# The inputs of the attention loaded at the end of a period, and one pair's sums made a period later

## The chip, the core and the metric

The kernel runs on one core of a Trainium2 chip. The metric is device time in microseconds (us). Before the change the median of three runs is 1099.42 us (1099.28 to 1099.94). The execution that the profiler recorded, from which all rows below come, took 1100.56 us; its first to its last instruction span 1098.8 us of that.

## The reference

Retention attention with 4 batches, 8 heads, 768 positions and a head size of 64, and two feed-forward layers over its 3072 tokens (model size 512, hidden size 2048), all in fp32:

```python
for t in range(S):
    state = gamma * state + einsum('bhd,bhe->bhde', k[:, :, t], v[:, :, t])
    y[:, :, t] = scale * einsum('bhd,bhde->bhe', q[:, :, t], state)
x = y.transpose(0, 2, 1, 3).reshape(B * S, H * D)
h = x @ w_in;  g = maximum(0.01 * h, h);  x = g @ w_out
h = maximum(x @ w_in2, 0);                out = (h * h) @ w_out2
```

## The kernel before

TensorE multiplies numbers split into a high and a low part, so that a product takes three matmuls (high by high, low by high, high by low). From the second block of tokens on, the products of a layer are done with seven products of half-size quarters instead of eight; the sums and differences of quarters of a weight that this takes are called its units. They are made once on VectorE (DVE) and ScalarE (ACT), written to DRAM and read back by the blocks that use them.

The tokens go in three blocks of 1024 (b = 0, 1, 2). A layer's 2048 hidden columns go in eight **periods** (q = 0 to 7) of two tiles of 128. Layer 0 of blocks 0 and 1 is interleaved with the attention of the positions that the later blocks need. One call of attend() in a period scores one pair of heads of a batch, finishes the values of the pair before it, prepares the next one and has the one after that loaded. Names in the rows:

- r: the loaded q, k and v of a pair (load_pair, two DMAs out of the input named first, three buffers each); vs and qs are its scaled parts (L193 on ACT, L183 on DVE), sc its scores, y its values, xs the values turned into the input of the layer.
- sg and st: raw weights in 64-bit words; L402, L403 on ACT and L404, L405, L408 on DVE turn them into fp32. In block 0 a period takes two sg tiles.
- wraw, wflt: fp32 weights kept in DRAM by block 0. In block 1 load_in(q + 2) loads wf from wraw (one buffer), and L506 on ACT and L507 on DVE split it and its sums (L520 to L523) into wa and wb. wid holds the units stored for later blocks; read_out(q + 1) loads wo, the units of the second product's weights, from wou.
- pa, pb, pd, acc: PSUM tiles. L716 copies the products of the first matrix, L742 to L756 add and activate them, and gh, gl (L797, L798) are the activated values that the second product (acc) takes.
- of: units of layer 1's second weights. make_units (L619) reads a pair of hidden tiles from wflt, all_units writes four plain quarters (L596 on ACT, L597 on DVE, wou on the GpSimd queue) and sum_units the four sums (L606 to L609, then L596 and L597 again). both_block (L958) steps these generators between the products of layer 1.

TensorE's instructions, every load (SyncE's queue, SP) and every store (GpSimd's queue, POOL) are pinned in the order in which the program is written: mm, load and store (L130 to L137) each wait for the one before on their queue. An issue whose buffer isn't free holds all that stand behind it on its queue. What ACT and DVE do is put in order by a scheduler that works on a model of the time, so a changed load can also change their order; on the chip both engines then take it in that order.

In block 0 the period ends with load_w (one or two sg); in block 1 with load_in and read_out. The loads of a pair's r are issued inside attend, ahead of those.

Of the kernel before, what the change touches and what calls it, by code (L numbers as in the profile page):

```python
# [30 lines left out]
NQ = NJ // 2  # L31
# [31 lines left out]
def retention_then_two_mlps(  # L63
# [66 lines left out]
    def mm(**kw):  # L130
        pin(nc.tensor.matmul(**kw))  # L131

    def load(**io):
        pin(nc.sync.dma_start(**io))
# [165 lines left out]
    n_load, n_prep, n_score, n_done = [0], [0], [0], [0]  # L300

    def loads_to(n):
        while n_load[0] < min(n, len(ups)):
            load_pair(ups[n_load[0]])
            n_load[0] += 1
# [19 lines left out]
        if last:  # L325
            prep_to(n_score[0] + 1)

    def attend(last):

        n, prev = n_score[0], ups[n_done[0]]  # L330
        if n < last:
            prep_to(n + 1)
            scores(ups[n], False, prev if n_done[0] < n and prev[0] < (NC - 1) * B else None)
            n_score[0] += 1
        if n_done[0] < n:
            values(prev)
            n_done[0] += 1
        prep_to(min(n_score[0] + 1, last))
        loads_to(min(n_done[0] + 3, n_score[0] + 2))

# [15 lines left out]
    def load_w(q, half):  # L358
        if q == NQ:
            return  # L360
        t = stage[q, half] = w_p.tile([P, 1024], U64, tag="sg", name="sg", bufs=2)
        load(out=t, in_=w1[q, half])
# [589 lines left out]
    def both_block(lay, b, here):  # L952

        nl, nb = (lay, b + 1) if b + 1 < NB else (1, 0) if not lay else (None, None)
        pa = None
        for n in range(NQ + 1):
            f = first_half(lay, b, n) if n < NQ else iter(())
            r = second_half(lay, b, n - 1, pa) if n else iter(())  # L958
            if (lay, b) == (1, 0) and 3 <= n <= 6:
                with aside():  # L960
                    next(here[n // 5], None)
            if (lay, b) == (1, 0) and n == NQ - 1:
                with aside():
                    next(made, None)
            for k in range(4):
                pa = next(f, None)
                if n == NQ - 1 and k < 2:
                    read_stage(lay, 0, (2 * k, 2 * k + 1))
                if lay == 0 and n and (k == 1 or k == 3 and n in (1, 2, 4, 5)):
                    with aside():  # L970
                        next(here, None)
                if k < 3:
                    next(r, None)
            if n == NQ - 1:
                read_stage(lay, 1, range(4))
            for q, k in UNITS[0 if not lay else 1 if b else 2].get(n, ()):
                read_units(lay, q, k)
            if (lay, b) == (1, 0) and n < NQ - 1 and n != 5:
                if n == 0:
                    v = quarters() + scratch("ss", "ss", "wb", "wf")  # L980
                else:
                    with aside():
                        next(made, None)
                if n in (0, 2, 4):
                    made = make_units(5 + n // 2, *v[:5])
                    next(made)
                    if n == 0:
                        here = [units_here(4, v[5], v[7]), units_here(6, v[6], v[5])]
                        for m in here:
                            next(m)  # L990
        A = [ps["acc"].tile([P, T], F32, tag=f"acc{m}", name="acc") for m in range(2)]
        s = {}
        steps = None if nl is None else operands(nl, nb)
        at = {4: (7, 13), 5: (5, 11), 6: (1, 5, 9)} if lay else {4: (13,), 5: (5, 11), 6: (1, 4, 8, 12)}
        for n, i in enumerate(STAGES):
            if i in (5, 2):
                Dd = [ps["acc"].tile([P, T], F32, tag=f"acc{2 + m}", name="acc") for m in range(2)]
            bank = Dd if i in (5, 3, 2) else A
            if i == 4:
                order = [(q, m) for m in range(2) for q in range(NQ)]  # L1000
            else:
                order = [(q, m) for q in range(NQ) for m in range(2)]
            for e, (q, m) in enumerate(order):
                r = rot[i, q]
                for k, (l, h) in enumerate(((0, 0), (1, 0), (0, 1))):
                    mm(
                        out=bank[m], lhsT=units[i, q // 2][:, q % 2, l, m * P:(m + 1) * P], rhs=r[:, h],
                        start=i in (1, 5, 2) and q == 0 and k == 0, stop=q == NQ - 1 and k == 2, skip_group_check=True,
                    )
                if e % 2 and n + 1 < len(STAGES):  # L1010
                    prepare(STAGES[n + 1], q)
                if e == 1:
                    if 1 <= n <= 5:
                        read_stage(lay, n + 1, range(4))
                    if n == (1 if lay else 3) and nl is not None:
                        read_x(nb)
                    if n in (3, 5) and lay and nl is not None:
                        read_units(1, (n - 3) // 2)
                    if n == 6 and nl is not None:
                        read_units(1, 2, 0, True)  # L1020
                if lay == 0:
                    if (n, e) in ((0, 1), (0, 9), (0, 15)):
                        with aside():
                            next(here, None)
                    if (n, e) in ((1, 1), (2, 13)):
                        made = units_here(n - 1, x_p.tile([P, 1024], F32, tag="xh4", name="of"))
                        next(made)
                    if n in (2, 4) and e in (3, 9):
                        with aside():
                            next(made, None)  # L1030
                if steps and e in at.get(n, ()):
                    with aside():
                        next(steps, None)
            if i in (1, 5):
                s[i] = late["r"].tile([P, 2, T], F32, tag="ss", name="ss", bufs=2)
            elif i == 6:
                s[i] = x_p.tile([P, 2, T], F32, tag="xl4", name="ss")
            elif i == 4:
                s[i] = w_p.tile([P, 2, T], F32, tag="wb", name="ss")
            for m in range(2):  # L1040
                if i in (1, 5, 6) or (i == 4 and m == 0):
                    nc.scalar.copy(s[i][:, m], bank[m])
                elif i == 4:
                    nc.vector.tensor_copy(s[i][:, m], bank[m])
                else:
                    y = s[{3: 6, 7: 5, 2: 1}[i]][:, m]
                    nc.vector.tensor_tensor(out=y, in0=y, in1=bank[m], op=ALU.add)
            if i in (3, 7, 2, 4):
                y, mh, t = {3: (s.get(6), 0, 1), 7: (s.get(5), 1, 1), 2: (s.get(1), 0, 0), 4: (s.get(4), 1, 0)}[i]
                for m in range(2):  # L1050
                    put = load if not lay or nl is None and i == 4 else store
                    put(out=(out if lay else ydr)[b][:, 2 * mh + m, t * T:(t + 1) * T], in_=y[:, m])
# [115 lines left out]
    for b in range(NB - 1):  # L1168
        rest = (b + 2) * B * NP
        for q in range(NQ):  # L1170
            more = 0 < q < NQ - 1
            if b == 0:
# [13 lines left out]
                emit_plain(q, 1, 1)  # L1186
                if more:
                    put_out(b, 2 * q - 1)
                attend(rest)
            else:  # L1190
                part = emit_in(0, b, q)
                next(part)
# [5 lines left out]
                    next(new, None)  # L1198
                if more:
                    put_out(b, 2 * q - 1, (0, 6))  # L1200
                attend(rest)
                next(part)
                with aside() if q and q > 6 else ExitStack():
                    next(new, None)
# [4 lines left out]
                    pass  # L1209
            if q + 1 < NQ:  # L1210
                if b == 0:
                    loads_to(n_done[0] + 3)
                    if q:
                        plain_in(q + 1)
                        if q + 2 < NQ:
                            load_w(q + 2, 0)
                        for n in (q - 1,) if q < 5 else (4, 5) if q == 5 else (6,):
                            out_sums(n)
                    with aside(), tc.issue_after(paired[q]):
                        make_out(q + 1)  # L1220
                    if q + 2 < NQ:
                        if q == 0:
                            load_w(q + 2, 0)
                        load_w(q + 2, 1)
                else:
                    if q + 2 < NQ:
                        load_in(q + 2)
                    read_out(q + 1)
            elif b == 0:
                out_sums(NQ - 1)  # L1230
            if b == 0 and q > 1:
# [117 lines left out]
```

## Time and profile before

| | |
|---|---|
| median of three runs | 1099.42 us |
| profiled execution | 1100.56 us, span 1098.8 us, mean granted TensorE clock 0.997 |
| TensorE busy | 1082.4 us, 99% of the span |
| VectorE busy | 763.4 us, 69% |
| ScalarE busy | 611.6 us, 56% |
| moved by DMA | 293.31 MB, 267 GB/s over the span |

Busy time of TensorE is as long as its matmuls at the clock that was granted, so a matmul at half the clock counts as busy for longer. Of ACT and DVE a third to a half is idle; that they are idle in the mean does not say that they are in time at a given place.

### The profile page before, as it was taken

Reading aid. Unit: us, or ns where it says so; the run is one execution under the profiler, and the core shown is the slowest. Engines: PE = TensorE matmul, PEld = TensorE weight load, DVE = VectorE, ACT = ScalarE, POOL = GpSimd, SP = SyncE. Lnnn points to the kernel's source line nnn. Section 1 sums busy time; section 2 is a strip of 40 time slices with the busy share of each in tenths; the row PEclk is TensorE's granted clock in tenths of the full one; section 3 lists DMA queues with packets and bytes.
Section 4 is the critical chain, followed back from the end, with each engine's and each line's share of the span. In section 5 each row is a group of like instructions: output and inputs, shape, how many; then the busy total and the mean of one; then the engine's idle time right before and its main releaser. Section 6 shows DMA issues by size and latency. Waiting matters only on the chain.

```text
span 1098.8 us, 15540 instructions
## 1 busy us (share of the span) xinstructions
PE 1082.4 (99%) x5599; PEld 862.5 (78%) x5599; DVE 763.4 (69%) x1333; ACT 611.6 (56%) x1111; POOL 87.2 (8%) x146
## 2 busy tenths in 40 slices
PE   9999999999989999999999999999999999999998
PEld 6787787777767777787788887888888888888886
DVE  5888997676755656658797968877555868456853
ACT  5757775554545554357665567655455555455542
POOL 0011111101000000012101012100000001000000
PEclk9999999999989999999999999999999999999999
DMA  9689998878797957679978778978335876447571
GB/s 373 211 332 331 355 337 311 290 267 298 249 341 247 344 202 248 231 289 377 375 265 290 287 264 278 399 261 344 116 135 198 318 255 230 155 148 260 167 241 58
DMA packets 81660, 293.31 MB, mean 267 GB/s; under 512 B 8368, under 2 KB 10928, under 8 KB 74032
## 3 DMA queue, kind: packets, MB, share of 16 engines
q1 hardware_dynamic: 62400, 214.00, 54.9%
q0 software_dynamic: 19040, 78.13, 18.3%
q8 instruction: 44, 0.72, 0.3%
q14 instruction: 32, 0.26, 0.1%
q10 hardware_dynamic: 144, 0.20, 0.1%
HBM read 206.31 MB, written 85.98 MB: 266 GB/s over the span
## 4 chain that ended last, share of the span: by engine, by line
PE 83%; DMA 6%; DVE 5%; issue 3%; ACT 2%; POOL 1%; SPq 0%; POOLq 0%; DVEq 0%; ACTq 0%
PE acc L131 40%; PE pa L131 23%; PE pd L131 7%; PE y L131 5%; PE pb L131 4%; PE sc L131 4%; DMA of<-wflt 2%; DMA wb<-wid 1%; DMA wf<-wraw 1%; DMA wid<-wa 1%; DMA wflt<-sf 1%; DVE rot L877 1%; PE idle L131 1%; DVE wa L507 0%; DVE xl L673 0%
## 5 line engine op out<-in xcount | busy, mean ns | idle before, releaser
L131 PE MATMUL acc<-rot,wu 128*128 128x512 f32 x1344 | 314.3, 395 | 0.0
L131 PEld LDWEIGHTS acc<-rot,wu 128*128 128x128 f32 x1344 | 252.3, 188 | 61.3
L131 PE MATMUL pa<-xh,wa 128*128 128x512 f32 x464 | 143.7, 391 | 0.0
L876 ACT CAST rot<-gu 128x512 fp32r<-128x512 f32 x160 | 99.0, 620 | 77.1 <-PE acc L131 67.8
L877 DVE TENSOR_TENSOR rot<-gu,rot 128x512 fp32r<-128x512 f32 x160 | 109.1, 688 | 46.7 <-ACT rot L876 46.1
L131 PE MATMUL pa<-xh,wb 128*128 128x512 f32 x432 | 135.9, 395 | 4.3 <-DVE wb L432 2.3
L131 PE MATMUL acc<-gh,wo 128*128 128x512 f32 x400 | 107.4, 401 | 3.8 <-ACT gh L797 3.8
L131 PEld LDWEIGHTS pa<-xh,wa 128*128 128x128 f32 x464 | 87.1, 188 | 19.5 <-DMA wa<-wid 0.4
L131 PE MATMUL pd<-xh,wa 128*128 128x512 f32 x320 | 99.0, 390 | 1.8 <-DVE wa L507 1.5
L131 PEld LDWEIGHTS pa<-xh,wb 128*128 128x128 f32 x432 | 79.7, 188 | 24.7 <-DVE wb L432 2.6
L131 PEld LDWEIGHTS acc<-gh,wo 128*128 128x128 f32 x400 | 75.1, 190 | 22.9 <-ACT gh L797 4.6
L131 PE MATMUL pa<-xl,wa 128*128 128x512 f32 x232 | 90.5, 390 | 0.0
L131 PE MATMUL pa<-xl,wb 128*128 128x512 f32 x216 | 84.2, 390 | 0.0
L131 PEld LDWEIGHTS pd<-xh,wa 128*128 128x128 f32 x320 | 60.0, 188 | 15.2 <-DVE wa L507 1.9
L877 DVE TENSOR_TENSOR rot<-gt,rot 128x512 fp32r<-128x512 f32 x64 | 44.2, 691 | 30.7 <-ACT rot L876 30.3
L131 PE MATMUL pd<-xl,wa 128*128 128x512 f32 x160 | 62.3, 389 | 0.0
L876 ACT CAST rot<-gt 128x512 fp32r<-128x512 f32 x64 | 39.6, 621 | 39.0 <-PE acc L131 36.2
L131 PE MATMUL acc<-gl,wo 128*128 128x512 f32 x200 | 57.7, 396 | 0.0
L723 ACT ACTIVATE gt<-gt 128x512 f32<-128x512 f32 x48 | 30.4, 633 | 47.7 <-DVE gt L904 33.1
L798 DVE TENSOR_TENSOR gl<-g,gh 128x512 fp32r<-128x512 f32 x50 | 34.1, 688 | 30.5 <-ACT gh L797 14.7
L916 DVE TENSOR_TENSOR gu<-gu,pb 128x512 f32<-128x512 f32 x32 | 22.0, 687 | 44.1 <-PE pb L131 44.0
L131 PEld LDWEIGHTS pa<-xl,wa 128*128 128x128 f32 x232 | 43.5, 188 | 9.2
(152 smaller groups left out, 1715.4 us busy)
## 6 DMA issues: line engine op xcount, KB each, us to landing
wu<-wou SPq DMA_DIRECT2D x112, 512.0 KB, 6.1
wa<-wid SPq DMA_DIRECT2D x28, 1024.0 KB, 6.0
wou<-of POOLq DMA_DIRECT2D x48, 512.0 KB, 6.5
wb<-wid SPq DMA_DIRECT2D x28, 768.0 KB, 6.5
wo<-wou SPq DMA_DIRECT2D x20, 1024.0 KB, 6.5
sg<-w SPq DMA_DIRECT2D x16, 1024.0 KB, 7.3
r<-first SPq DMA_DIRECT2D x50, 256.0 KB, 5.7
st<-w SPq DMA_DIRECT2D x24, 512.0 KB, 7.6
```

The source lines that it names most:

```text
L131: pin(nc.tensor.matmul(**kw))
L723: nc.scalar.activation(out=g, in_=g, func=AF.Relu)
L798: mark[1] = seq(nc.vector.tensor_tensor(out=gl, in0=g, in1=gh.bitcast(F32), op=ALU.subtract)).ins
L876: mark[0] = nc.scalar.copy(r[:, 0], s).ins
L877: mark[1] = nc.vector.tensor_tensor(out=r[:, 1], in0=s, in1=r[:, 0].bitcast(F32), op=ALU.subtract).ins
L916: nc.vector.tensor_tensor(out=u[:, 0], in0=u[:, 0], in1=pb, op=ALU.add)
```

## The change

Two edits. First, attend takes the number of pairs to load ahead as an argument; in the periods of blocks 0 and 1 it is 2 and not 3, so that attend there issues no load, and the loads of the next pair come at the end of the period: behind load_w in block 0, behind load_in and read_out in block 1 (not in the last period of a block). Second, in layer 1 of block 0 the step of make_units is left out in n = 4 and not in n = 5, and the generator for pair 7 starts in n = 5 and not 4, so that the last sums of pair 6 are made one period later.

```diff
-    def attend(last):
+    def attend(last, more=3):
...
-        loads_to(min(n_done[0] + 3, n_score[0] + 2))
+        loads_to(min(n_done[0] + more, n_score[0] + 2))
...
-            if (lay, b) == (1, 0) and n < NQ - 1 and n != 5:
+            if (lay, b) == (1, 0) and n < NQ - 1 and n != 4:
...
-                if n in (0, 2, 4):
+                if n in (0, 2, 5):
                     made = make_units(5 + n // 2, *v[:5])
...
-                attend(rest)
+                attend(rest, 2)
             else:
...
-                attend(rest)
+                attend(rest, 2)
...
                 if b == 0:
-                    loads_to(n_done[0] + 3)
                     if q:
                         plain_in(q + 1)
...
                         load_w(q + 2, 1)
+                    loads_to(n_done[0] + 3)
                 else:
                     if q + 2 < NQ:
                         load_in(q + 2)
                     read_out(q + 1)
+                    loads_to(n_done[0] + 3)
```

No matmul, cast or byte is added or taken away, and TensorE's order is the same. On SP the loads stand in another order. In block 0 the two r of a period go behind its two sg:

```order
-L134 DMA r<-first 128x512 x2
-L134 DMA sg<-w 128x1024 x2
-L134 DMA st<-w 128x512
-L134 DMA r<-first 128x512 x2
-L134 DMA sg<-w 128x1024 x2
+L134 DMA sg<-w 128x1024 x2
+L134 DMA r<-first 128x512 x2
+L134 DMA st<-w 128x512
+L134 DMA sg<-w 128x1024 x2
+L134 DMA r<-first 128x512 x2
```

The sg loads of a period are now issued ahead of its r. In block 1, from the first period on (wraw_105 and the wo behind it), the two r go behind wf and wo:

```order
-L134 DMA r<-first 128x512
-L134 DMA r<-first 128x384
 L134 DMA wflt_0_112<-sf 128x512
 L134 DMA wf<-wraw_105 128x1024
 L134 DMA wo<-wou_123 128x4x512
+L134 DMA r<-first 128x512
+L134 DMA r<-first 128x384
 L134 DMA wflt_0_118<-sf 128x512
 L134 DMA st<-w 128x512
 L134 DMA wf<-wflt_0_106 128x512
-L134 DMA r<-first 128x512
-L134 DMA r<-first 128x384
```

So the r of a period is three issues later on the queue, and the next wf and wo are no longer behind it. On ACT the order in the first period of block 1 is the one of before, but for the r that vs names (r_2801 before, r_2851 now); this is the order now:

```order
L743 ACTIVATE g_2749<-g_2749 128x512
L193 ACTIVATE vs_2956<-r_2851,tab0_78 128x64 x2
L747 ACTIVATE g_2749<-g_2749 128x512
L402 ACTIVATE sf_2815<-st_2648 128x512
L403 ACTIVATE st_2648<-st_2648 128x512
L752 ACTIVATE g_2740<-g_2740 128x512
L756 ACTIVATE g_2840<-pa_2733 128x512
L506 CAST wa_2914<-wf_2846 128x256
L797 CAST gh_2830<-g_2740 128x512
```

Between vs and the gh that the second product takes stand six other instructions. In later periods of block 1 the scheduler puts vs behind the copies of the next tile, and the first cast of the next wf (L506) ahead of xs. On DVE, in layer 1 of block 0, where the sums of pair 6 (L606 to L609, L597) and the units wa and wb (L507) meet, before:

```order
L522 TENSOR_TENSOR of<-of 128x2x128
L726 SCALAR_TENSOR_TENSOR gu<-gu 128x512
L597 TENSOR_TENSOR of<-of 128x2x256
L523 TENSOR_TENSOR of<-of 128x2x128
L877 TENSOR_TENSOR rot<-gu,rot 128x512
L926 SCALAR_TENSOR_TENSOR gu<-pa,gu 128x512
L904 TENSOR_TENSOR gt<-gt,pd 128x512
L919 TENSOR_TENSOR gu<-gt,gu 128x512
L507 TENSOR_TENSOR wb<-of,wb 128x2x256
L507 TENSOR_TENSOR wb<-of,wb 128x2x128
L507 TENSOR_TENSOR wa<-of,wa 128x2x384
```

and now:

```order
L522 TENSOR_TENSOR of<-of 128x2x128
L523 TENSOR_TENSOR of<-of 128x2x128
L916 TENSOR_TENSOR gu<-gu,pb 128x512
L726 SCALAR_TENSOR_TENSOR gu<-gu 128x512
L507 TENSOR_TENSOR wa<-of,wa 128x2x384
L877 TENSOR_TENSOR rot<-gu,rot 128x512
L606 TENSOR_TENSOR of<-of 128x256
L919 TENSOR_TENSOR gu<-gt,gu 128x512
L926 SCALAR_TENSOR_TENSOR gu<-pa,gu 128x512
L607 TENSOR_TENSOR of<-of 128x256
L507 TENSOR_TENSOR wb<-of,wb 128x2x256
```

The large wa (128x2x384) now comes ahead of the sums and ahead of rot, and the sums follow it. On POOL the store of this wa moves ahead of two stores of units and of the load of pair 7 from wflt.

## Rows read from the trace of the kernel before

**Rows 1.** The page's part on busy time and share of each engine.
```profile
PE 1082.4 (99%) x5599; PEld 862.5 (78%) x5599; DVE 763.4 (69%) x1333; ACT 611.6 (56%) x1111; POOL 87.2 (8%) x146
```
**Rows 2.** Waits of TensorE: who was waited for, us in total, times, longest.
```profile
PE acc L131 <- ACT gh L797: 3.8, 1, 3.8
PE pa L131 <- DVE wb L432: 2.3, 1, 2.3
PE pd L131 <- DVE wa L507: 1.5, 1, 1.5
```
**Rows 3.** Chain of waits, 255 to 330 us: start, length, what.
```profile
273.67 2.78 PE acc L131 x12
...
301.70 9.48 DMA wf<-wraw
...
312.44 5.49 PE acc L131 x12
```
**Rows 4.** Busy time by stretch and engine; PEclk, DMA share and GB/s end the row.
```profile
94.00:98.00 4.00, 3.76 (x16) 3.10 (x17) 3.93 (x6) 0.60 (x1) 0.00 (x0) 1.00 0.89 320
310.00:320.00 10.00, 7.56 (x22) 6.03 (x23) 5.14 (x10) 5.20 (x10) 1.05 (x2) 0.66 1.03 414
```
**Rows 5.** Timeline of SP's queue: start, time held at the issue, what.
```profile
64.96 7.95 SPq L134 DMA_DIRECT2D r<-first  x2
73.09 0.66 SPq L134 DMA_DIRECT2D sg<-w  x1
...
254.33 0.93 SPq L134 DMA_DIRECT2D r<-first  x2
...
259.39 0.37 SPq L134 DMA_DIRECT2D wo<-wou  x1
...
273.63 9.46 SPq L134 DMA_DIRECT2D r<-first  x2
...
285.61 0.39 SPq L134 DMA_DIRECT2D wf<-wraw  x1
...
290.06 10.50 SPq L134 DMA_DIRECT2D r<-first  x2
...
301.70 0.33 SPq L134 DMA_DIRECT2D wf<-wraw  x1
```
**Rows 6.** Timeline of ACT: start, busy us, what, idle before and what ended it.
```profile
82.92 1.12 ACT L402 ACTIVATE wf<-sg 128x1024 f32<-128x1024 f32 x1 [1.24 <-DMA sg<-w]
...
266.70 0.59 ACT L193 ACTIVATE vs<-r,tab 128x64 f32<-128x64 f32 x2 [0.41 <-PE sc L131]
268.99 0.63 ACT L747 ACTIVATE g<-g 128x512 f32<-128x512 f32 x1 [1.71 <-DVE g L746]
...
271.94 1.14 ACT L797 CAST gh<-g 128x512 fp32r<-128x512 f32 x2
...
311.25 0.62 ACT L506 CAST wb<-wf 128x512 fp32r<-128x512 f32 x1 [4.57 <-DMA wf<-wraw]
```
**Rows 7.** Timeline of DVE, columns as in rows 6.
```profile
66.39 1.22 DVE L408 CUSTOM_DVE_ANT_0 wf<-sg,wf 128x2048 uint16<-128x2048 uint16 x1
...
300.72 0.95 DVE L507 TENSOR_TENSOR wa<-wf,wa 128x768 fp32r<-128x768 f32 x1
...
681.55 0.69 DVE L597 TENSOR_TENSOR of<-of 128x512 fp32r<-128x512 f32 x1
...
685.83 0.95 DVE L507 TENSOR_TENSOR wa<-of,wa 128x768 fp32r<-128x768 f32 x1
```
**Rows 8.** Timeline of TensorE, the second product in block 1's first period.
```profile
273.51 0.63 PE L131 MATMUL acc<-gh,wo 128*128 128x512 f32 x2
```
**Rows 9.** Instructions on tile wo, 255 to 275 us: its load's time to landing.
```profile
DMA to landing us min/median/max: 12.7/12.7/12.7
```
**Rows 10.** Timeline of POOL in layer 1 of block 0.
```profile
683.25 0.55 POOL L137 DMA_DIRECT2D of<-wflt  x1
...
693.75 0.72 POOL L137 DMA_DIRECT2D wou<-of  x1 [5.60 <-DVE of L597]
```

## The prediction

> **What bounds the kernel now.** The share of busy time comes first: TensorE is busy for 1082.4 us, 99% of the span [rows 1]. No matmul is removed, so a gain can only come from its waits and from time in which it runs at half the clock. The table of its waits is next. Three entries can have to do with the change: 3.8 us for gh, 2.3 us for wb and 1.5 us for wa [rows 2]. The two short waits for g (L742) are behind nothing that moves, and I leave them where they are.
>
> For the wait for gh the chain of waits shows that a load of wf ends first (301.70, 9.48 us), and that the twelve matmuls behind it take 5.49 us where the same twelve at another place take 2.78 [rows 3]. [...] That wait therefore costs 3.8 + 5.49 - 2.78 = 6.5 us. The reader then goes from TensorE back to ACT, and from ACT to SP's queue, asking at each what came late.
>
> **The change part by part.**
>
> *A, loads in block 0.* SP issues r at 64.96 and is held there for 7.95 us, since the second r has no free buffer; the sg<-w behind it goes out at 73.09 only [rows 5]. Its own buffer was free from 66.39 + 1.22 = 67.6, when L408 had read the sg before it [rows 7]. ACT then sits idle until 82.92, when that sg lands [rows 6], and L402, L403 and the casts to wb follow in order; TensorE waits 2.3 us for wb. With sg ahead of r it can go out at about 67.7, 5.4 us earlier, more than twice the wait. The r behind it is pushed later by two sg; its vs is needed a period on. I count -2.3. Ends: 0 (sg lands no earlier because the DMA queues are full) to -2.3.
>
> *B, loads in block 1.* The wf at 301.70 stands behind an r that holds SP from 290.06 for 10.50 us [rows 5]. But its buffer, the only one, was also busy: DVE's L507 read it from 300.72 to 301.67 [rows 7]. So moving r past it gains nothing unless that L507 is earlier as well. It works on the wf issued at 285.61, and that one stood behind an r held from 273.63 for 9.46 us, to 283.09 [rows 5]. With both r behind their wf, the whole row of wf loads, casts and releases moves ahead by some 5 us a period. ACT's 4.57 us at 311.25, where it has a wf cast ahead of gh and waits for the load [rows 6], is then gone, and with it the 3.8 us and the half clock: -6.5. Ends: 0, if the buffer stays the limit, to -6.5. I take the full value, since 5 us is more than 3.8.
>
> *C, a new wait.* In block 1's first period r went out at 254.33, ahead of wf and of the wo at 259.39 [rows 5]; now it goes out behind that wo. ACT's order here is unchanged: vs at 266.70, which was waiting only for PE, then L747 at 268.99 and without a gap to gh at 271.94 [rows 6]. TensorE takes gh at 273.51 [rows 8], a slack of about 1 us. The wo took 12.7 us to land, until 272.1 [rows 9], since the stores of ydr and wid share the DMA engines. The same bytes are moved by then whether r goes first or last, so I put r's landing at 272.1. From there ACT needs vs (0.59), then from L747 to the end of the first gh 271.94 + 0.57 - 268.99 = 3.5, together 4.1: gh at 276.2, and TensorE waits 276.2 - 273.5 = 2.7, with 0.3 for gl, which DVE makes from gh: +3.0. Ends: 0, if r lands by 269.4, and 4.1, if its 0.46 MB come after wo's landing at 414 GB/s [rows 4], 1.1 us.
>
> [...]
>
> Whether this wait also halves the clock is open: the wait of 2.3 us did not (what follows it runs at 1.00 in the profile's page), the one of 3.8 us did [rows 2, 4]. At 3.0 I take no, and keep 2.7 us for the range.
>
> [...]
>
> *Other places where r is now late.* In later periods vs stands behind the next tile's copies on ACT, behind which gh doesn't wait; the cast of the next wf (L506) now stands ahead of xs and L747, and a late wf would hold gh again. The nearest rows are 0 (ACT waits for nothing there now) and the 4.57 of rows 6. The wf is some 5 us earlier, so I take 0.5. At the end of block 1 the last r is also behind a wo, with the first evacuation queued behind its vs: between 0 and C's 4.1, taken 0.4, since that wo has no wid stores beside it.
>
> *D, the sums of pair 6.* TensorE waits 1.5 us for DVE's L507 on wa, which runs from 685.83 to 686.78; one of the L597 of pair 6 stands ahead of it at 681.55 with 0.69 [rows 7]. Pair 6's four sums and two L597 ahead of it take some 2.6 us on DVE (starts 0.34 apart for the sums, 0.60 for L597). In the new order L507 on wa comes before all of them, and before L877 and the products behind it, so it is ready more than 2 us earlier: -1.5. Ends: 0 and -1.5. What is late next: the load of pair 7 from wflt, issued at 683.25, now stands on POOL behind two stores of units, which wait for DVE's later L597; in the trace such a store goes out at 693.75 [rows 10], so it is some 10 us later. Its casts L596 come one period later on ACT with products of the same period behind them. Between 0 and 1.5 (the wait removed); I take 0.2.
>
> **Sum**, from the profiled execution's 1100.56: -2.3 - 6.5 - 1.5 + 3.0 + 0.5 + 0.4 + 0.2 = -6.2, so 1094.4. The median of the runs is 1.14 below the profiled one: 1093.2 us. About 0.2% (2.2 us) is what a measurement can tell from no change.
>
> **Rivals.**
> - *C does not come*: r overtakes wo or lands by 269.4. For it: at 254 to 256 the DMA engines have little to do, and wf goes out earlier. Against: wo itself took to 272.1. 1093.2 - 3.0 = 1090.2.
> - *C halves the clock*, or r lands at the upper end. For: 3.8 us did it. Against: 2.3 us did not. 1093.2 + 2.7 = 1095.9.
> - *B does not go*: the limit is wf's one buffer and not SP. For: the wf at 301.70 went out 0.03 us after DVE had let go of it. Against: DVE's cast was itself late by a wf that had stood behind r. 1093.2 + 6.5 = 1099.7, no change.
> - *Slower: r behind wo in every period of block 1.* SP now holds r until wo has a buffer, and r lands with it; if ACT comes to vs first, as in C, then gh is late each period, with the price of B, 3.8 + 2.7 = 6.5 each. Two such periods beside C decide: 1093.2 + 13 = 1106.2. For: wo's 12.7 us to landing, and one in-order ACT. Against: the new order has vs behind the next tile's copies from the second period on, and wid's stores come earlier.
>
> **Chances.** The forecast 0.46, C absent 0.12, C with the clock 0.15, B unchanged 0.13, slower 0.14. Faster by over 0.2% is below 1097.2: the first three, 0.73. Within 0.2%: 0.13 and a little of the slower case with one period instead of two, 0.15. Slower: 0.12. The range goes from C absent with a few tenths of the small terms gone, 1089.5, to B unchanged with the spread of that sum, 1100.5; left out are the slower case and little else.
>
> **What would show it.** A: no wait for wb near 92 us, sg at about 67.7. B: no wait for gh near 308, the clock 1.00 there, wf issued before 297. C: a wait for gh near 273.5 of 2 to 4 us, ACT idle ahead of vs until r lands at about 272. D: no wait for wa near 685. I am wrong if ACT waits for r in later periods and gh is late behind it, or if wf still goes out right behind L507 at its old time.

## The result

The changed kernel takes 1105.24 us (median of five runs, 1102.87 to 1109.05), the kernel before 1099.40. The ratio is 1.0059, 95% interval 1.0044 to 1.0074: slower by 0.6%, where 1093.2 was forecast and 1100.5 was the upper end of the range. The profiled execution is the fastest of the five, 1102.87 us with a span of 1101.1, so its trace shows 2.3 us of the loss and not the whole of it; the trace of before is of an execution 1.2 us above its median.

TensorE's waits after, to be laid beside [rows 2] (who was waited for, us in total, times, longest):

```profile
PE acc L131 <- ACT gh L797: 4.6, 3, 3.2
PE pa L131 <- DVE gt L911: 2.8, 2, 2.3
PE sc L131 <- DVE g L742: 2.2, 2, 1.8
...
PE pa L131 <- ACT gu L895: 1.2, 1, 1.2
PE pa L131 <- DVE g L746: 1.1, 1, 1.1
PE acc L131 <- ACT wo L431: 0.8, 1, 0.8
```

The waits for wb and wa of [rows 2] are gone, the one for gh is not the same one, and there are new ones. Since TensorE does the same instructions in the same order, the start of each in one trace less its start in the other tells where time was lost. This is that difference, after less before, by place (worked out from the two traces, times of the trace of before):

```
start of the program       -1.20   (not put down to the change: -0.9 to 0.0 in the six runs below that leave block 0's loads alone)
 94  wait for wb gone       -2.61
188 to 208  end of block 0  +2.73
273 to 288  first period of block 1, wait for gh and half clock  +5.33
290 to 307  second and third period   +1.59
307 to 320  old wait for gh and its half clock gone  -5.83
332  fourth period          +1.31
354 to 360  short waits     -1.05
392  last periods           +1.58
400 to 560                  +0.02
630 to 690  wait for wa gone  -2.17
705  wait for gt            +2.60
sum                         +2.30
```

The three waits that the change could remove did go; six other places gave back more. The waits at the new places, on TensorE's timeline after (start, busy us, what, and the wait before it):

```profile
185.90 2.46 PE L131 MATMUL acc<-gh,wo 128*128 128x512 f32 x8 [0.81 <-ACT wo L431]
...
275.83 0.73 PE L131 MATMUL acc<-gh,wo 128*128 128x512 f32 x2 [3.24 <-ACT gh L797]
...
310.05 0.73 PE L131 MATMUL pa<-xh,wb 128*128 128x512 f32 x2 [1.14 <-DVE g L746]
...
333.78 2.11 PE L131 MATMUL acc<-gh,wo 128*128 128x512 f32 x8 [1.07 <-ACT gh L797]
...
394.32 0.71 PE L131 MATMUL sc<-r 64*128 64x128 f32 x6 [1.79 <-DVE g L742]
...
707.95 0.73 PE L131 MATMUL pa<-xh,wb 128*128 128x512 f32 x2 [2.31 <-DVE gt L911]
```

For the first large one, SP's queue after, and ACT behind it (compare [rows 5, 6], where r went out at 254.33 and vs ran at 266.70 with 0.41 us of idle time before it):

```profile
258.31 0.37 SPq L134 DMA_DIRECT2D wo<-wou  x1
258.74 1.34 SPq L134 DMA_DIRECT2D r<-first  x2
```

```profile
271.74 0.59 ACT L193 ACTIVATE vs<-r,tab 128x64 f32<-128x64 f32 x2 [6.53 <-DMA r<-first]
...
275.15 1.15 ACT L797 CAST gh<-g 128x512 fp32r<-128x512 f32 x2
```

ACT stands still for 6.53 us in front of vs, and gh comes 3.4 us after vs starts. The clock is halved for a part of what follows (granted 0.50 from 278 to 280; columns as in [rows 4], the last but two is the granted clock):

```profile
275.00:280.00 5.00, 4.17 (x12) 3.02 (x13) 4.93 (x12) 3.68 (x8) 0.00 (x0) 0.75 0.66 208
280.00:285.00 5.00, 5.00 (x22) 3.80 (x22) 1.96 (x3) 2.05 (x3) 1.06 (x2) 0.91 0.78 211
```

In the third and fourth period of block 1 it is a cast of the next wf that holds ACT, in the third ahead of xs and L747, in the fourth ahead of gh (ACT's timeline after):

```profile
308.05 0.62 ACT L506 CAST wb<-wf 128x512 fp32r<-128x512 f32 x1 [5.12 <-DMA wf<-wraw]
308.58 0.36 ACT L290 COPY xs<-y 128x256 f32<-128x256 f32 x1
310.03 0.63 ACT L747 ACTIVATE g<-g 128x512 f32<-128x512 f32 x1 [1.09 <-DVE g L746]
...
331.28 0.41 ACT L506 CAST wa<-wf 128x256 fp32r<-128x256 f32 x1 [2.92 <-DMA wf<-wraw]
...
333.11 1.14 ACT L797 CAST gh<-g 128x512 fp32r<-128x512 f32 x2
```

At 308 the order on DVE adds to it: L507 on that wb stands ahead of L746, which TensorE waits for. The load that ACT waits for there, and DVE's last reading of its buffer before it (SP and DVE after, beside 301.70 in [rows 5] and 300.72 in [rows 7]):

```profile
300.73 0.32 SPq L134 DMA_DIRECT2D wf<-wraw  x1
```

```profile
299.75 0.95 DVE L507 TENSOR_TENSOR wa<-wf,wa 128x768 fp32r<-128x768 f32 x1
```

The load still goes out 0.03 us behind L507 (299.75 + 0.95 = 300.70), 1.0 us earlier than before, and takes 7.2 us to land where it took 9.5. So ACT's wait for it was not shorter (5.12 us, 4.57 before); it stands at another place in ACT's order.

In layer 1 the load of pair 7 goes out at 692.41 where it went out at 683.25 [rows 10], and ACT, then DVE, wait for it (POOL, ACT and DVE after):

```profile
692.41 0.55 POOL L137 DMA_DIRECT2D of<-wflt  x1
```

```profile
700.14 1.14 ACT L596 CAST of<-of 128x512 fp32r<-128x512 f32 x2 [1.50 <-DMA of<-wflt]
```

```profile
700.79 0.69 DVE L597 TENSOR_TENSOR of<-of 128x512 fp32r<-128x512 f32 x1 [1.22 <-ACT of L596]
...
707.22 0.68 DVE L911 TENSOR_TENSOR gt<-gt,pa 128x512 f32<-128x512 f32 x1
```

From 700.79 DVE works without a gap, and three sums and three L597 stand among the gt and gu that TensorE needs, ahead of that L911; gt is 2.3 us late.

### The profile page after: what moved, and what is told of

Its sections match the earlier page's. It is cut to its first block, busy times and chain, and to the rows that moved or that the text cites. A ratio compares the mean times of both kernels' runs of the same rounds, so it can differ in the third digit from the quotient of the medians.

```text
span 1101.1 us, 15512 instructions
## 1 busy us (share of the span) xinstructions
PE 1081.5 (98%) x5599; PEld 861.1 (78%) x5599; DVE 764.4 (69%) x1333; ACT 612.4 (56%) x1111; POOL 87.3 (8%) x146
## 4 chain that ended last, share of the span: by engine, by line
PE 87%; DMA 6%; DVE 3%; ACT 2%; issue 1%; SPq 0%; POOL 0%; ACTq 0%; DVEq 0%
PE acc L131 43%; PE pa L131 24%; PE pd L131 8%; PE y L131 5%; PE pb L131 4%; PE sc L131 3%; DMA r<-first 2%; DMA wf<-wraw 1%; DMA wb<-wid 1%; DMA of<-wflt 1%; DMA wid<-mc 1%; PE idle L131 1%; DVE of L597 0%; DVE gu L916 0%; ACT gh L797 0%
## 5 line engine op out<-in xcount | busy, mean ns | idle before, releaser
L798 DVE TENSOR_TENSOR gl<-g,gh 128x512 fp32r<-128x512 f32 x50 | 34.1, 688 | 26.2 <-PE acc L131 13.5
```

The source lines that it names most:

```text
L798: mark[1] = seq(nc.vector.tensor_tensor(out=gl, in0=g, in1=gh.bitcast(F32), op=ALU.subtract)).ins
```

## The experiments

Each is compared with runs of the kernel before that were taken together with it on the same chip (1100.48 us beside the first four, 1099.84 beside the next four, 1099.71 beside the last two). Gains in us are worked out from the ratio unless the medians are named. The first four take the change apart.

**Block 0's loads alone** (in its periods attend loads nothing, and r goes out behind load_w).

```diff
-                attend(rest)
+                attend(rest, 2)
...
+                    loads_to(n_done[0] + 3)
```

> Only the loads of block 0 are moved (attend(rest, 2) and the loads at the end of the period in block 0; block 1 and the sums as before). Theory 1, each edit pays at its own place: the wait for wb near 92 us goes (-2.6), and the end of block 0 gives it back (+2.7, from the cast to wo that ACT now takes behind gh, and from the pair loads that slip behind wo), so 1099 to 1100 us, no change. Rival, the end of block 0 is late only because of what block 1's loads do to the order: 1096.8 us and no new wait between 185 and 210.

1099.09 us, ratio 0.9978 (0.9963 to 0.9993): it gains some 2.4 us (1.4 by the medians), where theory 1 had no change and the rival -2.6. In size the rival is nearer, but its account is out: the trace has the new wait for wo at 186 (0.81, as in the changed kernel), which the rival puts down to block 1's loads. By place this trace wins 2.6 us near 94 and loses 2.2 at the end of block 0, much as theory 1 has it. What the rest of the gain is, isn't shown. One possible part: behind the same wait for wb near 94 the trace of before has a granted clock of 1.00, and that of sums_only, which doesn't touch block 0's loads, the row below; the place costs 1.6 us more there, and without the wait that is saved too.

```profile
94.00:99.00 5.00, 5.00 (x16) 3.91 (x17) 4.03 (x5) 0.60 (x1) 0.00 (x0) 0.66 0.52 203
```

**Block 1's loads alone** (the same behind load_in and read_out).

```diff
-                attend(rest)
+                attend(rest, 2)
...
                     read_out(q + 1)
+                    loads_to(n_done[0] + 3)
```

> Only the loads of block 1 are moved (behind load_in and read_out); block 0 and the sums as before. Theory 1: the first period's wait for gh with the clock halved (+5.4), the casts of the next wf ahead of xs and L747 (+1.5 near 308, +1.3 near 333) and the late vs near 392 (+1.4), against the removed wait near 308 with its half clock (-5.8) and some -0.5 of short waits: +3.3, so about 1102.7 us. Rival, only the first period's wait counts and the others come from the shift that the other edits bring: +5.4 - 5.8 - 0.5, so 1098.5 us.

1104.87 us, ratio 1.0036 (1.0022 to 1.0050): slower by some 4 us, theory 1's side. Its trace has the wait for gh at 276.73 (3.02) with a granted clock of 0.72 from 275 to 280, three more for gh of 0.3 to 1.6, and 1.72 for L742 near 396. Behind that last one the clock is halved as well, which it isn't behind the 1.79 at 394 in the execution of the changed kernel (1.00 from 396 to 401); the place costs 2.9 us here and 1.4 there.

```profile
396.00:401.00 5.00, 5.00 (x33) 3.75 (x34) 1.38 (x4) 0.91 (x2) 0.00 (x0) 0.66 0.98 315
```

**The sums alone.**

```diff
-            if (lay, b) == (1, 0) and n < NQ - 1 and n != 5:
+            if (lay, b) == (1, 0) and n < NQ - 1 and n != 4:
...
-                if n in (0, 2, 4):
+                if n in (0, 2, 5):
```

> Only the sums of pair 6 one period later (n != 4 and n in (0, 2, 5)); all loads as before. Theory 1: the wait for wa near 685 goes (-1.6), and the load of pair 7, now behind two stores on POOL, lands near 700 and holds L596 on ACT, so that DVE comes late with gt near 706 (+2.6): about 1100.4 us. Rival, as predicted at first (-1.5 + 0.2): 1098.1 us, and the wait near 706 belongs to the moved loads.

1103.13 us, ratio 1.0025 (1.0013 to 1.0038). Slower, and by more than theory 1's 1.0: in this execution TensorE waits 3.1 us for gt near 705, and the clock is halved behind it, so that the place costs 5.0 us against the changed kernel's 2.6. The half clock near 94 adds 1.6, which has nothing to do with the sums.

```profile
PE pa L131 <- DVE gt L911: 3.6, 2, 3.1
```

```profile
705.00:710.00 5.00, 4.56 (x13) 3.64 (x14) 3.79 (x7) 2.77 (x5) 0.91 (x2) 0.66 0.90 313
```

**Both blocks' loads, not the sums.** The diffs of the first two together.

> Both blocks' loads moved, the sums as before. Theory 1, the edits add up: the changed kernel less the +1.0 of the sums, so about 1.0 below it: 1104.2 us beside its median of 1105.2, and no wait near 706, the wait for wa near 685 back. Rival, the loads alone are worth what was predicted less the half clock: -2.3 - 6.5 + 5.4 + 0.9, so 1096.9 us, and the sums carry the loss.

1102.62 us, ratio 1.0015 (1.0002 to 1.0027), slower than before; the rival is out, and theory 1's number is missed too: the loads alone are 2.6 us below the changed kernel by the medians, not 1.0. The ratios of the two blocks add up: -0.22% and +0.36% make +0.14% (measured 0.15%). With the sums' +0.25% that is some 0.4%, just below the interval of the whole change (0.44 to 0.74).

The next four go at the causes.

**The first period's r as before**, in block 1 of the kernel with block 1's loads alone; so in the next two.

```diff
-                attend(rest, 2)
+                attend(rest, 2 if q else 3)
```

> As b1_only (1104.9 us), but in block 1's first period attend loads r itself, ahead of wf and wo as before (attend(rest, 2 if q else 3)); ACT's order stays that of b1_only. Theory 1: the r behind wo is the whole cause of the wait for gh near 276 and of the half clock behind it, 5.0 us together, and the later places keep theirs: 1099.9 us. Rival: the wait covers the later ones, since every other engine gains 5 us on TensorE in it, so that without it the casts of the next wf are late by more: 1102.5 us or above, with waits near 292, 315 and 335 that sum to over 5 us.

1100.57 us, ratio 1.0012 (1.0001 to 1.0022), beside 1.0036 with r behind wo. The wait at 276 is gone, so r behind wo makes it, but only 2.6 of the 5.0 us came back (3.7 by the medians). The profiled execution is the slowest of the ten, 1104.14 us, so its short waits are not those of the median. The wait for L746 near 290 grew from 0.47 to 1.42, and two short ones near 359 and 377 came up, so the rival has its part: the first wait hid some of the later ones. The waits it names sum to 3.6, not over 5.

**r behind wf, ahead of wo.**

```diff
                         load_in(q + 2)
+                    loads_to(n_done[0] + 3)
                     read_out(q + 1)
-                    loads_to(n_done[0] + 3)
```

> As b1_only, but r between load_in and read_out: behind wf, ahead of wo. Theory 1: r lands some 6 us after wf's issue and ahead of wo's bytes, so the wait near 276 goes (-5.0) and the late vs near 392 too (-1.3); the casts' waits stay: 1098.6 us. Rival, r is late because the DMA engines are full there and not because of its place behind wo: ACT still waits for r until about 270 and the time is 1103 us or more.

1098.94 us, ratio 0.9985 (0.9972 to 0.9997), as theory 1 has it within 0.4 us; the rival is out. r goes out ahead of wo, vs no longer waits for it, and the wait of a cast for wf is left (SP and ACT of this kernel):

```profile
258.12 0.90 SPq L134 DMA_DIRECT2D r<-first  x2
...
260.06 0.38 SPq L134 DMA_DIRECT2D wo<-wou  x1
```

```profile
267.36 0.59 ACT L193 ACTIVATE vs<-r,tab 128x64 f32<-128x64 f32 x2 [0.41 <-PE sc L131]
...
287.31 0.41 ACT L506 CAST wa<-wf 128x256 fp32r<-128x256 f32 x1 [5.97 <-DMA wf<-wraw]
```

**The casts of the next wf held behind gh**, that is behind L797 and L798 of the period before.

```diff
+                held = list(mark)
...
-                with aside() if q and q > 6 else ExitStack():
+                with aside() if q > 6 else ExitStack() as hold:
+                    if 1 < q < 7:
+                        for i in held:
+                            hold.enter_context(tc.issue_after(i))
                     next(new, None)
```

> As b1_only, but from the third period on the first casts of the next wf (L506) may not come on ACT ahead of the gh of the period before (issue_after on its L797 and L798); the loads stay. Theory 1: the short waits for g (L746) and gh near 292 to 335, 2.7 us together, come from casts that stand on ACT ahead of xs and L747 and wait for wf: 1102.2 us. Rival: wf itself is too late, and the wait moves to wb on TensorE: 1104.9 us, no change.

1099.72 us, ratio 0.9999 (0.9987 to 1.0011), against 1.0036 without the hold: the order in which ACT took the casts cost some 4 us, more than the 2.7 that I counted, since the wait near 396 shrank too (1.72 to 0.43) and the half clock behind it went (the next pairs of 128x512 matmuls take 0.73 and 0.62 us, where the first behind the 1.60 in loads_only takes 1.22). No wait for wb took their place; the wb in the list is block 0's, as in [rows 2]. What stays is the first period's wait for gh, which this kernel doesn't touch:

```profile
PE acc L131 <- ACT gh L797: 3.9, 1, 3.9
PE pa L131 <- DVE wb L432: 2.3, 1, 2.3
...
PE pd L131 <- DVE wa L507: 1.3, 1, 1.3
PE sc L131 <- DVE g L742: 1.3, 3, 0.5
```

**The later sums without the load of pair 7.**

```diff
-                    made = make_units(5 + n // 2, *v[:5])
-                    next(made)
+                    made = make_units(5 + n // 2, *v[:5]) if n < 5 else all_units(7, *v[:5])
+                    if n < 5:
+                        next(made)
```

> As sums_only (1103.1 us), but pair 7 is made from what lies in the buffer, without its load from wflt, so its units hold pair 6's numbers; this lets the scheduler place its casts earlier as well. Theory 1: the load that lands near 700, and the casts and sums bunched behind it, make gt late near 705 (3.1 us and a half clock behind it): without it that wait goes, 1099 us. Rival: two lots of sums in one period overload DVE whether or not the load is late: the wait near 705 stays at 2 us or more and the time at 1102 us or more.

1097.71 us, ratio 0.9986 (0.9976 to 0.9996). The wait near 705 is gone, and the whole is faster than before by about the wait for wa: two lots of sums in one period are not in themselves too much for DVE. The late load is the cause, by its landing or by the order that the scheduler makes of it; the two are not told apart.

Last, the mends together.

**Both blocks' loads with both mends of block 1**, sums as before.

> The loads of both blocks at the end of the period as in loads_only, the sums as before, with two mends in block 1: r behind wf but ahead of wo, and from the third period on the first casts of the next wf not ahead of the gh of the period before. If the causes add up: block 0's -1.4 to -2.4, and in block 1 the removed wait near 308 with its half clock (-5.8) with neither the wait near 276 nor those of the casts: 7.2 to 8.2 us below the kernel before, so 1091.6 to 1092.6 beside 1099.8. If instead each cure uncovers the next wait, as the removed one did in the changed kernel, it comes out at 1096 us or above.

1095.23 us, ratio 0.9954 (0.9942 to 0.9966): 4.5 us faster than before by the medians and the best of all. It is short of the sum of its parts and below the rival's 1096, so neither is met. The mean granted clock of its execution is 1.0, the end of block 0 still loses 2.6 us in it, and these waits are left:

```profile
PE sc L131 <- DVE g L742: 2.3, 4, 1.2
PE idle L131 <- DVE zero L1060: 1.5, 1, 1.5
PE acc L131 <- ACT wo L431: 0.8, 1, 0.8
PE pd L131 <- DVE wa L507: 0.7, 1, 0.7
```

No wait is left near 308. Its wf goes out later than before there, at 302.69, again 0.03 us behind L507, but lands after 5.1 us instead of 9.5, and gh stands ahead of the cast (SP and ACT of this kernel):

```profile
302.69 0.32 SPq L134 DMA_DIRECT2D wf<-wraw  x1
```

```profile
307.15 1.13 ACT L797 CAST gh<-g 128x512 fp32r<-128x512 f32 x2
308.75 0.61 ACT L506 CAST wb<-wf 128x512 fp32r<-128x512 f32 x1
```

So an earlier issue of wf is not what removed the wait. The shorter landing and the order on ACT are not told apart: no run holds the casts with the loads as before.

**The same, with the end of block 0 as before.**

```diff
-                attend(rest, 2)
+                attend(rest, 2 if q < 5 else 3)
```

> As both_loads_mended, but in block 0 attend loads r itself again from the sixth period on (attend(rest, 2 if q < 5 else 3)), so that ACT casts wo ahead of gh at the block's end as before. If the 1.5 to 2.7 us lost between 185 and 208 come from that order of ACT and from the r that slip behind wo: 1.5 us or more below both_loads_mended, 1090.5. If they come from block 0 being ahead by 3.8 us of loads that have their own time: the same as both_loads_mended.

1098.11 us, ratio 0.9978 (0.9968 to 0.9987), slower than the one without, so neither account's number. ACT casts wo ahead of gh again and the wait at 186 is gone, but a wait of 3.4 us for wb comes up near 170:

```profile
PE pa L131 <- ACT wb L431: 3.4, 1, 3.4
```

By it TensorE comes 5.4 us later to the end of block 0 than in the kernel without this edit. So this settles nothing there: the edit moved the order of the whole stretch.

## Why the prediction was wrong

The step that failed is the one on what is late next. The sum followed each moved load to the instruction that uses it and gave the rest small prices: *other places* 0.9, pair 7's load 0.2, the clock in C and the end of block 0 nothing. The runs showed 4.5, 2.6, 2.3 and 2.7 us there. In block 1's later periods the cause is shown: ACT's new order has casts that wait for a load ahead of what TensorE needs. The clock in C is in every run with r behind wo; for pair 7's load, its landing and the order are not told apart, and the end of block 0 is read from traces alone.

- *A* was right: -2.3 forecast, -2.6 in the trace. The sg went out at 65.3 us and not 73.1, and ACT had it at 77.9 and not 82.9. The end of block 0, +2.7, was in no step. I had taken each r to be needed a period on, and had not asked what the new loads do to the scheduler's order: ACT's cast to wo (L431) now comes behind a gh, and TensorE waits 0.81 for it; that place makes 1.4 of the 2.7. Another 0.65 goes in front of an acc that waits for y (L831) at 193, and 0.6 at scores near 206, whose cause stays open. That the cast's place is the cause of the 1.4 is read from the trace; the one run that tried it made another wait.
- *B* came out near in size, -6.5 forecast and -5.8 measured, but not by its step, and so in part by luck. The half clock was there (granted 0.50 from 312 to 318 in the trace of before) and went (1.00 from 310 to 320 after). The wf was to go out some 5 us earlier, before 297, and ACT's wait for it to vanish. It went out at 300.73, right behind L507's reading of its one buffer and 1.0 us earlier, which is the condition of the rival *B does not go*, and ACT waits for it longer than before. It did land 3.3 us earlier, since the load took less time; and TensorE comes to that place 5.8 us later than before, by the losses ahead of it, so that a part of the wait is hidden behind them.
- *C* was right as a wait: r landed at 271.7 (272.1 forecast), gh was taken at 275.83, 3.24 us of waiting (3.0). The upper end, r 1.1 us behind wo's landing (0.46 MB at 414 GB/s), was 273.2; the trace has r 1.5 us earlier. I had put wo's 12.7 us down to the stores that share the DMA engines with it (busy for 0.97 of the time from 259 to 272 in the trace of before); beside stores of the same tiles wo took 8.3 with r behind it, so the stores alone don't explain the 12.7. The clock was the wrong choice: it was halved, and the place cost 5.3. Every run with r behind wo in that period has it (waits of 2.85, 3.02, 3.24 and 3.86 us; granted clocks of 0.72, 0.75 and 0.70 over 5 us behind the last three). This was a rival with 0.15. The ground against it, that the wait of 2.3 us near 94 had not halved the clock, held for that one execution: in sums_only, b1_r_before_wo and b1_no_hoist the same wait was followed by a half clock (0.66 from 94 to 99).
- *Other places where r is now late*, 0.9 in the sum, is where the step failed in block 1. They came to 1.59 + 1.31 + 1.58 = 4.5 us in the trace. I had seen that casts of the next wf stand ahead of xs and L747, and took 0.5 near the lower end because wf was to be some 5 us earlier. It went out 1.0 us earlier, and the casts wait 5.12 and 2.92 us for it with what TensorE needs behind them. b1_no_hoist takes these casts back and some 4 us go. That the scheduler moved them up because its model has wf land earlier is my reading; no run shows the model's times. The wait at 394 is for L742, one of the two that the prediction left where they were.
- *D* was right for the wait removed (-1.5, measured -2.2) and wrong on what is late next: 0.2 was taken for pair 7's load and 2.6 was measured, above the upper end of 1.5. I had the load 10 us later (it was 9.2) and stopped there; I didn't follow it to DVE, where the units of pair 7 then fall among the products of the same period. In sums_no_load the load is gone and the wait with it.
- The slower rival that I wrote down, r behind wo in every period, is not what happened: in block 1 ACT waited for r in the first period (6.53 us) and again near 354, 371 and 389 (0.6 to 1.5), and not at 298, 317 and 337; at the end of block 0 it waited 1.8 us at 200.

Against the forecast of -6.2 the trace has +3.5 without the start: the clock in C 2.3, the casts and late loads 3.6, the end of block 0 2.7, and D's successor 2.4, less 1.3 on the other terms. The median is another 2.4 us above the profiled execution. Which of the places vary from run to run isn't shown by one profile. Two candidates come from other kernels' executions: the wait near 705, 3.1 us with a half clock in the sums alone where the changed kernel's has 2.3 without (0.66 from 705 to 710 there, 1.00 from 707 to 712 here), and the one near 394, with a half clock behind it in b1_only and not here (0.66 and 1.00 from 396 to 401).

## What to carry to other kernels

Where a scheduler orders two engines by a model of the time, a load that is moved earlier in the queue can change that order, and the engine in front can then wait for the load with other work behind it, as ACT did here for 5.12 and 2.92 us; look in the new order for the instructions that moved up because of the load, and give each the wait that it would have if the load lands as late as the trace shows. A load put behind a large one has to be followed to the first in-order instruction that needs it. When a wait like the 2.3 us near 94 or the 1.6 to 1.8 near 395 remains, price it with the half clock behind it as well as without: that one execution kept its clock behind such a wait (1.00 near 94 before) does not say that the next will (0.66 in sums_only).

## What the runs showed of the hardware

A load of 0.46 MB issued right behind one of 1 MB on SP's queue, beside stores on GpSimd's queue (issued from 257.1 to 260.4), took 10.1 and 12.3 us to land for its two parts, where the same loads ahead of it had taken 5.7 and 5.8 us in the trace of before. The load of 1 MB took 8.3 us in front and 12.7 behind. So in these two traces the pair was down at about the same time (271.7 and 272.1), and the one that stood behind on the queue came last.

The length of a wait of TensorE did not by itself tell whether a stretch at half the clock followed (0.50 from 312 to 318 in the trace of before). All waits of 2.85 us and more were followed by one, in each trace that has such a wait (a granted clock of 0.50 to 0.75 over some 5 us). The wait of 2.27 to 2.35 near 94 was in three traces (0.66 from 94 to 99 in sums_only, b1_r_before_wo and b1_no_hoist) and not in two (1.00 in before and b1_only). The wait near 395 was in three (1.60 us in loads_only, 1.72 in b1_only and b1_q0_before) and not in the changed kernel (1.79).
